# A stage-one load, a softmax and a clearing set earlier or later in a written order, and a scratch layout turned round

## The chip, the cores and the metric

The kernel runs on one core of a Trainium2 chip. The metric is the device time of one execution in microseconds; lower is better. Five engines work from queues of their own and in order: TensorE (PE; its weight loads are listed apart as PEld), VectorE (DVE), ScalarE (ACT), GpSimd (POOL) and the sync engine (SP), which here issues every DMA. An engine whose next instruction waits stands still, and so does everything behind that instruction in its queue.

## The reference

Three layers, one after the other, in float32:

```python
X = np.fft.rfft(x, axis=1)                                   # x: 8 batches, 3072 tokens, 256 channels
y = np.fft.irfft(X * (filt_r + 1j * filt_i)[None], n=3072, axis=1)
h = y.reshape(24576, 256) @ w_in                             # 256 -> 2048
z = (h / (1 + np.exp(-h))) @ w_out                           # SiLU, 2048 -> 256
logits = z @ phi                                             # 32 slots = 8 experts x 4
d = softmax(logits, axis=0)                                  # over all 24576 tokens
slot = d.T @ z
slot_out = [np.maximum(slot[e] @ w1[e], 0) @ w2[e] for e in range(8)]
out = softmax(logits, axis=1) @ slot_out                     # "combine"
```

## The kernel before

The 24576 tokens are worked in 48 chunks of 512, six to a batch. A chunk's main work is 16 hidden blocks: `hidden` (six matmuls into `ph`), `act` (ACT makes `g` with SiLU) and `turn` (DVE transposes `g` into `X`). From `g` come the logits (`pl`), from the logits an online softmax over all tokens (`soft0` to `soft3`), whose exponentials `e` go through DRAM (`spread0` stores `ed`, `spread1` loads it as `E`, line 669). `dsum` multiplies `E` with `X` into four PSUM banks (`pd`), and `update` on DVE adds them to `acc` (line 688), which frees the banks. Every four chunks a second, per-token softmax for the combine is made: `cprep` (DVE), `cexp` (ACT), `cfin` (DVE, lines 707 to 712, then a store of `cT`, line 714).

Beside these chunks the Fourier convolution of the next batch is worked in stages by `fft_plan(b, t0)`, during the six chunks of batch b-1:

- stage one, 12 steps u: `load1` (x and a piece c of the matrix), `split1` (ACT copies c into `ch`, line 286; DVE and POOL split both into high and low parts, lines 287 to 291), `mat1` (`pa`), and stores into a first scratch `s1`. The first `split1` stands in the last chunk of batch b-2, just before that chunk ends;
- stage two, four visits Q: `load2` reads `s1` as `a`, `mat2` makes `px`, ACT, DVE and POOL multiply with the filters f into y;
- stage three, `mat3` (`pb`), `out3` copies it to `eb` and `store2` writes it to a second scratch `s2` (line 265);
- stage four per chunk: `load3` reads `s2` as b (lines 540 to 542), `fly` adds and subtracts its halves on DVE, `mat4` makes `py`, and `out4` the tokens `yT` that `hidden` starts from.

Batch 0 has its own function, `fft_first`, before everything else.

Nothing schedules this: every step is put into a list with a time, `at(t, step)`, in which one hidden block is 1 and a chunk 16. The list is sorted and written out, and each engine's queue follows it (`manual_schedule`). Two times per chunk gather the small matmuls: `VIS1` = 1.9 (`pb`, the second half of the logits, `px`) and `VIS3` = 10.9 (`pd`, the first half of the logits, `py`). The instructions after that list, the tail with the experts and the output, are placed by the framework; so is the memset of the tile `sim` (line 883). A tile pool's tag has a number of buffers (`BUFS`), and a load waits until the buffer it gets is free. `px`, `pb`, `py` and `pd` share three PSUM banks (`pf`) with others.

## Time and profile before

| | us |
|---|---|
| median of 3 runs | 2019.61 (2015.79 to 2022.84) |
| the profiled execution | 2024.79 |
| its span, first to last instruction | 2023.0 |
| PE busy | 1872.3 |
| DVE busy | 1298.3 |
| ACT busy | 951.4 |
| POOL busy | 339.2 |
| mean granted TensorE clock | 0.951 of full speed |

The span is what the profile covers; the 1.8 us between it and the execution's own time lie before and after. Busy time of the engines overlaps. A granted clock of 1.00 is 2.4 GHz and 0.50 is 1.2 GHz, the two levels that the records show; a value between is a mixture of both within the stretch.

### The profile page before, as it was taken

The page shows a single profiled execution, that of the slowest core. Times are in us where ns is not written, and L with a number is a line of the kernel's source. Part 1 is how long each engine was busy: PE and PEld are TensorE (multiplying, and loading weights), DVE is VectorE, ACT ScalarE, POOL GpSimd, SP SyncE. Part 2 cuts the span into 40 slices and gives each one's busy share as a digit, 9 for nine tenths or more (in the row PEclk, how much of TensorE's full clock was granted, in tenths as well). Part 3 has the DMA queues.
Part 4 walks back from the last instruction along what each step waited for, and adds up shares of the span by engine and source line. Part 5 has one row for each costly group of instructions (what it writes and reads, how often), then busy time and mean ns, then how long its engine had stood idle before and what let it go on. Part 6 is the DMA issues. An engine that isn't in the chain of part 4 may idle for free. (4 is left out here: it accounts for less than half of the span.)

```text
span 2023.0 us, 49877 instructions
## 1 busy us (share of the span) xinstructions
PE 1872.3 (93%) x21108; PEld 1401.2 (69%) x21108; DVE 1298.3 (64%) x2207; ACT 951.4 (47%) x1816; POOL 339.2 (17%) x248
## 2 busy tenths in 40 slices
PE   4569999999999999999999999999999998999975
PEld 2158777877777777767776777767776776787643
DVE  5776665767676676767576675766576675555443
ACT  3444563554544554545544644544544544444323
POOL 3652220221121121221121211211121120000000
PEclk7679999999999999999999999999999999999996
DMA  9746442454254333553344524543254333301569
GB/s 277 212 157 185 112 113 81 144 135 118 58 178 124 92 97 96 166 134 81 90 145 125 126 63 127 155 114 80 77 159 124 95 94 106 108 24 46 182 240 386
DMA packets 196159, 264.36 MB, mean 131 GB/s; under 512 B 18784, under 2 KB 145120, under 8 KB 191712
## 3 DMA queue, kind: packets, MB, share of 16 engines
q1 hardware_dynamic: 195936, 261.17, 43.5%
q8 instruction: 166, 2.72, 0.6%
q14 instruction: 57, 0.47, 0.1%
HBM read 177.80 MB, written 83.30 MB: 129 GB/s over the span
## 5 line engine op out<-in xcount | busy, mean ns | idle before, releaser
L61 PE MATMUL ph<-yT,w_hl 128*128 128x512 f32 x4608 | 1107.3, 396 | 8.5 <-ACT g L594 6.9
L61 PEld LDWEIGHTS ph<-yT,w_hl 128*128 128x128 f32 x4608 | 859.3, 190 | 215.1 <-issue 28.3
L604 DVE STREAM_TRANSPOSE X<-g 128x512 f32<-128x512 f32 x768 | 521.0, 697 | 238.5 <-ACT g L594 238.1
L594 ACT ACTIVATE g<-ph 128x512 f32<-128x512 f32 x768 | 454.0, 607 | 347.5 <-PE ph L61 294.8
L237 POOL TENSOR_TENSOR sw<-sw,f 128x512 f32<-128x512 f32 x128 | 179.0, 1419 | 762.4 <-DMA ed<-e 230.0
L572 ACT ACTIVATE yT<-py 128x512 fp32r<-128x512 f32 x96 | 57.4, 598 | 361.2 <-PE py L61 361.2
L61 PE MATMUL pd<-X,E 32*32 32x512 f32 x6144 | 223.9, 604 | 3.0 <-issue 1.8
L61 PEld LDWEIGHTS pl<-g,wp 128*32 128x32 f32 x6144 | 164.4, 110 | 76.5 <-issue 58.9
L61 PE MATMUL pl<-g,wp 128*32 128x128 f32 x6144 | 193.2, 276 | 6.2 <-issue 6.0
L291 POOL TENSOR_TENSOR xh<-x,xh 128x512 fp32r<-128x512 f32 x84 | 111.5, 1328 | 495.2 <-DVE xh L290 426.1
L61 PEld LDWEIGHTS pd<-X,E 32*32 32x32 f32 x6144 | 119.5, 103 | 78.5 <-issue 41.8
L688 DVE SCALAR_TENSOR_TENSOR acc<-acc,nm,pd 128x512 f32<-128x512 f32 x188 | 126.9, 736 | 23.9 <-PE pd L61 23.9
L573 DVE TENSOR_TENSOR yT<-py,yT 128x512 fp32r<-128x512 f32 x96 | 66.3, 691 | 60.9 <-ACT yT L572 60.9
L61 PE MATMUL py<-d,b 128*128 128x128 f32 x416 | 72.6, 302 | 30.5 <-DVE acc L688 17.0
L361 DVE TENSOR_TENSOR y<-y,sw 128x512 f32<-128x512 f32 x112 | 98.1, 916 | 0.0
L61 PE MATMUL pa<-xh,ch 128*128 128x256 f32 x504 | 77.6, 288 | 18.2 <-ACT wp L146 9.8
L61 PE MATMUL px<-a,em 24*32 24x512 f32 (+1 forms) x1072 | 71.1, 642 | 23.6 <-DMA a<-s 17.6
L61 PEld LDWEIGHTS pa<-xh,ch 128*128 128x128 f32 x504 | 72.5, 193 | 28.6 <-ACT wp L146 10.0
L287 DVE TENSOR_TENSOR ch<-c,ch 128x256 fp32r<-128x256 f32 x84 | 42.8, 509 | 75.3 <-ACT ch L286 74.7
L226 ACT ACTIVATE sw<-px,sg 128x256 f32<-128x256 f32 x128 | 64.2, 501 | 47.1 <-DVE y L232 30.0
L61 PEld LDWEIGHTS py<-d,b 128*128 128x128 f32 x416 | 62.2, 214 | 34.8 <-DVE acc L688 18.6
L234 DVE TENSOR_TENSOR y<-px,f 128x512 f32<-128x512 f32 x120 | 78.7, 675 | 10.3 <-ACT sw L227 8.8
(126 smaller groups left out, 1305.9 us busy)
## 6 DMA issues: line engine op xcount, KB each, us to landing
f<-in_filt_dram SPq DMA_DIRECT2D x128, 256.0 KB
x<-in_x_dram SPq DMA_DIRECT2D x96, 256.0 KB
a<-s SPq DMA_DIRECT2D x128, 192.0 KB
s<-eb SPq DMA_DIRECT2D x128, 192.0 KB
out_dram<-ots SPq DMA_DIRECT2D x40, 512.0 KB
d<-in_dmat_dram SPq DMA_DIRECT2D x48, 256.0 KB
wt<-in_w_dram SPq DMA_DIRECT2D x12, 1024.0 KB
E<-ed SPq DMA_DIRECT2D x188, 64.0 KB
```

What stands on the lines that cost most here:

```text
L61: T.matmul(o, lhsT=l, rhs=r, start=start, stop=stop)
L226: A.activation(sw[:, 0, :], p[:, 1, :], AF.Copy, scale=sg[:, s:s + 1])
L234: V.tensor_tensor(y, p, f[:, 0, :].unsqueeze(1).to_broadcast([P, 2, CH]), op=ALU.mult)
L237: G.tensor_tensor(sw, sw, f[:, 1, :].unsqueeze(1).to_broadcast([P, 2, CH]), op=ALU.mult)
L287: V.tensor_tensor(ch[:, 1], c, ch[:, 0], op=ALU.subtract)
L291: G.tensor_tensor(h[:, 1, :], tf, h[:, 0, :], op=ALU.subtract)
L361: V.tensor_tensor(y, y, st.pop(("sw", Q, U)), op=ALU.add)
L572: A.activation(y[:, half, 0, :], py, AF.Copy)
L573: V.tensor_tensor(y[:, half, 1, :], py, y[:, half, 0, :], op=ALU.subtract)
L594: A.activation(g, pht.pop((c, m)), AF.Silu)
L604: V.transpose(xt[c][:, m].rearrange("p b j -> p (b j)"), gt[c, m])
L688: V.scalar_tensor_tensor(out=acc[:, :, a, :], in0=acc[:, :, a, :], scalar=mrun[c][:, 3:4], in1=p, op0=ALU.mult, op1=ALU.add)
```

## The change

Four things are changed, and the order of some steps with them.

1. In `fft_plan`, for all batches from 1 on, the first three `load1` are set nine, eight and seven times before the first `mat1`, the later ones up to seven before their own; c gets four buffers in place of two, and the tag `ev` one in place of two. `mat1` of steps 5, 6 and 7 move by up to a block.
2. The first visit of stage two (`tx`) of batches 2 to 7 moves from `t0 + 22.9` to `t0 + 27.1`, behind the `pd` and `py` of that time, as batch 1 has it already; its `load2` comes half a block earlier.
3. The combine softmax: `cfin` gets one of three places by its chunk, `cprep` another place at the end of a batch, and `cexp` is issued in whichever `soft2` comes next. The memset of `sim` gets a written place (`clear_sim`).
4. `s2` gets the layout of `s1`: `store2` writes 8 KB in one run per partition, `load3` reads pieces of 1 KB where it read 2 or 3 KB.

```diff
-            ld=3, c=2, ch=2, xh=2, ev=2, a=1, f=2, sw=1, y=2, ev8=1, bl=1, bp=1, dl=1, wt=3)
+            ld=3, c=4, ch=2, xh=2, ev=1, a=1, f=2, sw=1, y=2, ev8=1, bl=1, bp=1, dl=1, wt=3)
...
-        s2t[b] = s2 = dram.tile([64, 2, NJ, CH], F32, tag="s2", name=f"s2_{b}")
+        s2t[b] = s2 = dram.tile([NJ, 16, 4, 2, CH], F32, tag="s2", name=f"s2_{b}")
...
-            k = 16 * Q + 4 * U
-            DQ.dma_start(s2[k:k + 4].rearrange("k c r e -> r (k c) e"),
-                         ev[S * U:S * U + NJ].rearrange("r q c e -> r (q c) e"))
+            DQ.dma_start(s2[:, 4 * Q + U].rearrange("r q c e -> r (q c e)"),
+                         ev[S * U:S * U + NJ].rearrange("p q c e -> p (q c e)"))
...
-            t1, tx = [t0 + d for d in (-4.3, -3.1, -1.9, -0.7, 2.6, 4.1, 5.6, 7.1, 11.5, 12.6, 13.7, 14.8)], t0 + 22.9
-        at(t1[0] - 6, begin)
+            t1, tx = [t0 + d for d in (-4.3, -3.1, -1.9, -0.7, 2.6, 4.2, 6.4, 8, 11.5, 12.6, 13.7, 14.8)], t0 + 27.1
+        at(t1[0] - 10, begin)
...
-            at(max(t - 6, ts[u - 2] + 0.4) if u > 1 else t - 6, load1, u)
+            at(max(t - 7, ts[u - 3] + 0.4) if u > 2 else t1[0] - 9 + u, load1, u)
...
-            at(t1[-1] + 4.5 if Q == 0 else tp + 2, load2, Q)
+            at(t1[-1] + 4 if Q == 0 else tp + 2, load2, Q)
...
-        dma = DQ.dma_start(t[:, 0:n, :], s2.rearrange("k c r e -> (k c) r e")[:, r0:r0 + n, :])
+        dma = DQ.dma_start(t[:, 0:n, :], s2.rearrange("r u q c e -> (u q c) r e")[:, r0:r0 + n, :])
...
-            dma = DQ.dma_start(t[i::2, n:4, :], s2[:, 1 - i, r1:r1 + 4 - n, :])
+            dma = DQ.dma_start(t[i::2, n:4, :], s2.rearrange("r u q c e -> (u q) c r e")[:, 1 - i, r1:r1 + 4 - n, :])
...
-        if c % 4 == 0 and c // 4 - 1 in csm:
-            cexp(c // 4 - 1)
+        for k in sorted(csm.keys() - cdone):
+            cexp(k)
...
+    def clear_sim():
+        tail["sim"] = tail["tp"].tile([P, 2, NE * 36], F32, tag="sim", name="sim")
+        V.memset(tail["sim"], 0.0)
...
+    at(t + 40, clear_sim)
...
-            at(t3 + 4 if last else t1 + 11.2, cprep, c // 4)
+            at(t3 + 4 if last else t1 + (11.2 if (c + 1) % CPB else 19.1), cprep, c // 4)
...
-                at(t1 + 16 + 7.2, cfin, c // 4)
+                at(t1 + {1: 43.8, 3: 27.8, 5: 19.1}[(c + 2) % CPB], cfin, c // 4)
```

What this does to the queues, at three places. In the rows the numbers after a tile's name are its batch (or chunk) and step; the last one only counts tiles.

On SP, at the end of chunk 5, where stage one of batch 2 begins; before:

```order
L265 DMA s2_1_670<-eb_1_3_3019 24x8x256 x4
L653 DMA ed_4_3088<-e_4_3062 128x128
L669 DMA E_4_3110<-ed_4_3088 32x4x128 x4
L540 DMA b_6_3116<-s2_1_670 128x768
L542 DMA b_6_3116<-s2_1_670 64x256 x2
L278 DMA x_2_0_3122<-in_x_dram 128x2x256
L280 DMA c_2_0_3124<-in_cmat_dram 128x256
L278 DMA x_2_1_3136<-in_x_dram 128x2x256
L280 DMA c_2_1_3138<-in_cmat_dram 128x256
L531 DMA d_6_3140<-in_dmat_dram 128x512
L278 DMA x_2_2_3177<-in_x_dram 128x2x256
L280 DMA c_2_2_3179<-in_cmat_dram 128x256
```

And in the change:

```order
L264 DMA s2_1_648<-eb_1_3_3021 24x2048 x4
L277 DMA x_2_0_3079<-in_x_dram 128x2x256
L279 DMA c_2_0_3081<-in_cmat_dram 128x256
L652 DMA ed_4_3094<-e_4_3064 128x128
L277 DMA x_2_1_3097<-in_x_dram 128x2x256
L279 DMA c_2_1_3099<-in_cmat_dram 128x256
L277 DMA x_2_2_3111<-in_x_dram 128x2x256
L279 DMA c_2_2_3113<-in_cmat_dram 128x256
L716 DMA cT_86<-lall_0_1314 128x512
L668 DMA E_4_3130<-ed_4_3094 32x4x128 x4
L539 DMA b_6_3136<-s2_1_648 128x3x256
L541 DMA b_6_3136<-s2_1_648 64x256 x2
```

The loads of x and c for three steps, and the store `cT` of the combine softmax, now stand between the store of s2 and the load of E; before they stood behind E and b.

On DVE, in the same chunk (`X_5` are its turns, `cm_0` and `ct_0` the combine softmax, `ch` and `xh` the first split); before:

```order
L604 STREAM_TRANSPOSE X_5_2994<-g_5_6_3142 128x512
L604 STREAM_TRANSPOSE X_5_2994<-g_5_7_3152 128x512
L287 TENSOR_TENSOR ch_2_0_3162<-c_2_0_3124,ch_2_0_3162 128x256
L290 CAST xh_2_0_3165<-x_2_0_3122 128x512
L707 TENSOR_REDUCE cm_0_2951<-ct_0_2949 128x16
L708 TENSOR_SCALAR cm_0_2951<-cm_0_2951 128x16
L709 RECIPROCAL cm_0_2951<-cm_0_2951 128x16
L710 TENSOR_TENSOR ct_0_2949<-ct_0_2949,cm_0_2951 128x512
L712 STREAM_TRANSPOSE lall_0_1314<-ct_0_2949 128x512
L604 STREAM_TRANSPOSE X_5_2994<-g_5_8_3168 128x512
L555 SCALAR_TENSOR_TENSOR bp_6_3188<-b_6_3116,sg_79 128x256
```

And in the change:

```order
L603 STREAM_TRANSPOSE X_5_2994<-g_5_2_3085 128x512
L603 STREAM_TRANSPOSE X_5_2994<-g_5_3_3101 128x512
L709 TENSOR_REDUCE cm_0_2951<-ct_0_2949 128x16
L710 TENSOR_SCALAR cm_0_2951<-cm_0_2951 128x16
L711 RECIPROCAL cm_0_2951<-cm_0_2951 128x16
L712 TENSOR_TENSOR ct_0_2949<-ct_0_2949,cm_0_2951 128x512
L714 STREAM_TRANSPOSE lall_0_1314<-ct_0_2949 128x512
L603 STREAM_TRANSPOSE X_5_2994<-g_5_4_3121 128x512
L603 STREAM_TRANSPOSE X_5_2994<-g_5_5_3140 128x512
L603 STREAM_TRANSPOSE X_5_2994<-g_5_6_3152 128x512
L603 STREAM_TRANSPOSE X_5_2994<-g_5_7_3162 128x512
L286 TENSOR_TENSOR ch_2_0_3172<-c_2_0_3081,ch_2_0_3172 128x256
```

The softmax's closing steps went from behind the first `ch` and `xh` to a place four turns earlier.

On PE, around the first `px` of batch 2 in chunk 7 (its last rows, then the hidden blocks up to `pd`); before:

```order
L61 MATMUL px_2_02_4089<-a_2_0_4036,em_77 32x512
L61 MATMUL px_2_03_4090<-a_2_0_4036,em_77 32x512
L61 MATMUL px_2_00_4087<-a_2_0_4036,em_77 32x256 x3
L61 MATMUL ph_7_7_4112<-yT_7_3834,w_hl_75 128x512 x6
L61 MATMUL ph_7_8_4129<-yT_7_3834,w_hl_75 128x512 x6
L61 MATMUL ph_7_9_4152<-yT_7_3834,w_hl_75 128x512 x6
L61 MATMUL ph_7_10_4172<-yT_7_3834,w_hl_75 128x512 x6
L61 MATMUL pd_6_0_4186<-X_6_3478,E_6_4065 32x512 x4
```

And in the change, the rows from `py` of the same chunk to the beginning of `px`:

```order
L61 MATMUL py_8_0_4238<-d_8_4081,bp_8_4117 128x128 x2
L61 MATMUL py_8_0_4238<-d_8_4081,b_8_4065 128x128 x2
L61 MATMUL py_8_1_4243<-d_8_4081,bp_8_4117 128x128 x2
L61 MATMUL py_8_1_4243<-d_8_4081,b_8_4065 128x128 x2
L61 MATMUL ph_7_11_4253<-yT_7_3834,w_hl_75 128x512 x6
L61 MATMUL px_2_00_4260<-a_2_0_4017,em_77 32x256
```

`px` stood four hidden blocks ahead of `pd`, and now comes one block behind `py`.

## Rows read from the trace of the kernel before

The stretches are named after where they lie: A goes from `pd` of a batch's chunk 4 to `pd` of its chunk 5, B from there to `pd` of the next chunk 0, C from there to `pd` of chunk 1. Rows of windows read: stretch, its us, then busy us of PE, PEld, DVE, ACT and POOL with their instructions, the granted clock, the DMA share and GB/s.

**Rows 1.** Part 1 of the page: busy us (share of span) xinstructions.
```profile
PE 1872.3 (93%) x21108; PEld 1401.2 (69%) x21108; DVE 1298.3 (64%) x2207; ACT 951.4 (47%) x1816; POOL 339.2 (17%) x248
```

**Rows 2.** TensorE's waits: line, waited for, total us, times, longest.
```profile
PE py L61 <- DVE acc L688: 17.4, 8, 4.8
...
PE py L61 <- DMA b<-s: 12.2, 1, 12.2
```

**Rows 3.** Six stretches A, two shown and the sum: us, busy us, clock, DMA.
```profile
336.40:382.01 45.61, 40.72 (x417) 33.07 (x416) 32.57 (x68) 21.48 (x44) 11.40 (x9) 0.93 0.51 160
...
560.41:600.88 40.47, 38.66 (x417) 30.93 (x417) 30.13 (x63) 21.49 (x44) 11.42 (x9) 1.00 0.56 175
...
sum 261.22, PE 239.84 PEld 193.71 DVE 188.12 ACT 129.14 POOL 68.47; mean PE 39.97 PEld 32.28 DVE 31.35 ACT 21.52 POOL 11.41
```

**Rows 4.** A stretch of the last batch, same view.
```profile
1733.89:1766.07 32.18, 32.18 (x369) 25.40 (x368) 17.73 (x30) 13.96 (x24) 0.00 (x0) 1.00 0.32 101
```

**Rows 5.** TensorE's timeline, one `pa` in stage one: start, us, engine, line, op.
```profile
573.57 0.87 PE L61 MATMUL pa<-xh,ch 128*128 128x256 f32 x6
574.28 2.88 PE L61 MATMUL ph<-yT,w_hl 128*128 128x512 f32 x12
```

**Rows 6.** Timeline of four engines around 336 us; in brackets idle, releaser.
```profile
329.32 3.09 DVE L604 STREAM_TRANSPOSE X<-g 128x512 f32<-128x512 f32 x5 [2.20 <-ACT g L594]
...
330.48 1.91 SPq L669 DMA_DIRECT2D E<-ed  x4
...
334.80 0.60 SPq L280 DMA_DIRECT2D c<-in_cmat_dram  x1
...
336.40 4.46 PE L61 MATMUL pd<-X,E 32*32 32x512 f32 x128
...
338.56 0.42 ACT L286 ACTIVATE ch<-c 128x256 fp32r<-128x256 f32 x1 [5.53 <-DMA c<-in_cmat_dram]
...
339.68 0.68 DVE L707 TENSOR_REDUCE cm<-ct 128x16 f32<-128x512 f32 x1
...
342.21 0.71 DVE L712 STREAM_TRANSPOSE lall<-ct 128x512 f32<-128x512 f32 x1
...
346.97 0.80 PE L61 MATMUL py<-d,b 128*128 128x128 f32 x2 [4.22 <-DVE acc L688]
```

**Rows 7.** The sum over the six stretches B, same view as rows 3.
```profile
sum 249.77, PE 243.50 PEld 179.32 DVE 166.44 ACT 117.62 POOL 49.34; mean PE 40.58 PEld 29.89 DVE 27.74 ACT 19.60 POOL 8.22
```

**Rows 8.** TensorE's timeline, first `px` of batch 3.
```profile
633.81 4.37 PE L61 MATMUL px<-a,em 24*32 24x512 f32 x36 [0.50 <-DMA a<-s]
```

**Rows 9.** Two stretches C: batch 1 and batch 3.
```profile
192.97:232.92 39.95, 38.73 (x477) 27.32 (x476) 27.29 (x44) 21.33 (x44) 11.13 (x8) 1.00 0.62 147
645.65:680.75 35.10, 35.10 (x439) 26.27 (x438) 25.71 (x40) 18.62 (x36) 7.16 (x6) 1.00 0.42 107
```

**Rows 10.** TensorE's timeline inside stretch C of batch 1.
```profile
199.37 1.08 PE L61 MATMUL pl<-g,wp 128*32 128x128 f32 x32 [0.88 <-issue]
...
215.41 2.11 PE L61 MATMUL pb<-y,gm 32*32 32x512 f32 x22 [0.34 <-DVE y L361]
```

**Rows 11.** Two stretches from `pd` of a chunk 3 to the next.
```profile
975.13:1008.43 33.30, 33.30 (x401) 25.71 (x400) 17.62 (x30) 14.73 (x26) 0.00 (x0) 1.00 0.21 54
1660.31:1701.71 41.40, 35.41 (x401) 26.92 (x400) 22.15 (x40) 16.45 (x29) 0.00 (x0) 0.92 0.30 92
```

**Rows 12.** VectorE's timeline, the memset.
```profile
1687.75 0.54 DVE L883 MEMSET sim<- 128x576 f32 x1 [5.59 <-DMA s<-eb]
```

**Rows 13.** Windows inside a store of s2 and in the output.
```profile
772.00:776.00 4.00, 4.00 (x19) 3.33 (x18) 0.41 (x2) 3.94 (x7) 0.00 (x0) 1.00 0.73 172
1960.00:2000.00 40.00, 29.03 (x276) 20.72 (x274) 21.18 (x35) 17.59 (x34) 0.00 (x0) 0.75 1.01 397
```

**Rows 14.** Timeline of a chunk's middle: fly of b, and `py`.
```profile
682.27 0.75 DVE L555 SCALAR_TENSOR_TENSOR bp<-b,sg 128x512 f32<-128x512 f32 x1 [1.96 <-DMA b<-s]
...
687.26 0.71 PE L61 MATMUL py<-d,bp 128*128 128x128 f32 x4
```

More of the change, by code (lines that the diff above doesn't have):

```diff
@@ L699, in cprep @@
         csm[k] = (t, cm)
+    cdone = set()
     def cexp(k):
+        cdone.add(k)
         t, cm = csm[k]
@@ L880, in fftconv_moe_softmoe @@
         mm(pT[:, h, :], sib[:, h * P:h * P + P], fold[:, 0:S], True, True)
-    sim = tp.tile([P, 2, NE * 36], F32, tag="sim", name="sim")
-    V.memset(sim, 0.0)
+    sim = tail["sim"]
     V.tensor_copy(sim.rearrange("p h (e x) -> p h e x", x=36)[:, :, :, 0:4],
```

## The prediction

> **What bounds the kernel now.** I read the page's first part, then TensorE's waits, then its timeline, and from that the stretches between one chunk's token sums and the next (the names `pd`, which every chunk has once). PE is busy for 93% of the span [rows 1], so a gain can only come out of PE's idle time, out of matmuls that run slowly, or out of work that disappears; this change removes no matmul. The list of waits [rows 2] puts 17.4 us on `py` behind `acc` and 12.2 us on the very first `py` behind `b`, and it is misleading in one respect: it counts idle time, not what a wait costs. For that I compare stretches. A chunk of the last batch, where no FFT runs any more, takes 32.18 us from `pd` to `pd` at full clock with PE busy throughout [rows 4]. That is the floor. A stage-one step `pa` put between two hidden blocks adds 574.28 - 573.57 = 0.71 us [rows 5].
>
> Stage one of each of batches 2 to 7 begins near the end of a chunk 5, two batches ahead. Three stretches matter for each: A, from `pd` of chunk 4 to `pd` of chunk 5, with eight `pa`; B, from there to `pd` of the next chunk 0, with four `pa` and the first `px`; C, the one after. The floor of A is 32.18 + 8 x 0.71 = 37.86. The six A sum to 261.22 us [rows 3], 261.22 - 6 x 37.86 = 34.1 over. The first shown has a clock of 0.93, the second 1.00: where the wait is long the clock falls to the lower level as well, and the whole excess of the first (7.75 us) is 1.8 times its wait of 4.22. The floor of B is 32.18 + 4 x 0.71 = 35.02; the six sum to 249.77 [rows 7], 39.6 over, and that includes the first `px` itself.
>
> **Why A is late** [rows 6]. SP issues the E loads from 330.48 and the first c only at 334.80. ACT, which works in order, stands 5.53 us in front of its first `ch` until 338.56, and all its `g` behind that stand too. DVE then has `ch`, `xh`, the closing of a combine softmax (from 339.68 to 342.21 + 0.71, 3.2 us), the turns of the late `g` and the fly of b before the update of `acc`, although `pd` ended at 336.40 + 4.46 = 340.86. `py` needs the banks which that update frees: 346.97, 4.22 us late. Batches 2, 4 and 6 have the softmax there, the other three only the late c.
>
> **The change, part by part.**
> - First x and c ahead of E, and the softmax ahead of `ch`. c is issued six to seven us earlier, so ACT's stand goes, and DVE has its 3.2 us of softmax behind it before `pd` ends. What is late next: E. On SP six loads now stand between the e store and E; one x is 0.60 and one c 0.60 at most [rows 6], with the store's own issue before them, so E is ordered some 2.5 us later. In batches 2, 4 and 6 the store of the softmax (cT) stands ahead of E as well, and SP waits there for DVE. DVE begins its turns at 329.32, the softmax comes after two of five (3.09 / 5 = 0.62 each): 330.6, and takes 2.5 to 3.2 us: 333.1 to 333.8. With cT's and E's issue (1.91) E is fully ordered at about 335.5 to 336.1. The c row took 338.56 - 334.80 = 3.8 us from issue to use in a full queue; E's four parts then land between about 336 and 339, and `pd` wanted them at 336.40. Bounds 0 and 2.5 us, I take 1.0 for three batches, and 0.3 everywhere for what I don't see: 3 x 1.0 + 6 x 0.3 = 4.8. A gains 34.1 - 4.8 = **29.3** (this holds the sixth `pa`, now one block later, too).
> - First `px` joined. In B, PE had to wait for a (0.50 us in the row) and then ran 36 small matmuls in 4.37 us [rows 8]; a is now ordered before f and used nine us later. The combine softmax that was prepared in the middle of B in three of the batches (`cprep`) goes into the next chunk. I leave 0.3 a batch: B gains 39.6 - 1.8 = **37.8**. But the work comes back in C. Batch 1 has had this very order all along: `py`, one hidden block, `px`. Its C took 39.95 against 35.10 for one that has no first `px` in it [rows 9], 4.85 more, of which 0.88 is an issue wait in `pl` that isn't the visit's. That leaves 3.97: 1.83 of matmuls, about 1.6 because `pb` comes before its products y are ready [rows 10] (POOL's four cross products are the chain), and 0.5 unexplained. Bounds 3.5 and 4.85, I take 3.97: C loses 6 x 3.97 = **23.8**.
> - Clearing moved. The memset of the `sim` tile stands in DVE's queue in front of an online-softmax step, and there waits 5.59 us for a store that still reads the memory it clears [rows 12]; behind it stand the softmax, ACT's exp and every `g`. That stretch takes 41.40 us, one of the same kind 33.30 [rows 11]. Its new place is two chunks later, in front of one turn, when the last such store is long done; 0.54 us of DVE beside a busy PE costs nothing there. Gain **8.1**.
> - 8-KB runs. A store of s2 moves 4 x 192 KB at 172 GB/s with a DMA share of 0.73 in 1-KB pieces; the output, in pieces of 3 to 4 KB, runs at 397 at 1.01 [rows 13]. Per busy engine that is 14.7 and 24.6 GB/s. At the second rate 786 KB take 2.7 us in place of 4.6. In the loop that is hidden, since everything behind it has slack or is counted above. In the first batch it is exposed: nothing runs while the first `py` waits for store and load [rows 2]. Against the 1.9 us stands the load of b, in 1-KB pieces now: 524 KB at 14.7 x 16 = 235 GB/s take 2.2 us, at the better rate 1.3, so up to 0.9 back. Bounds -1.9 and +0.9; I take a gain of **1.0**. The row shows a store that never uses more than three quarters of the engines. The Trainium skill (DMA: Bandwidth & Descriptors, Why a DMA increments its semaphore by 16 and not by 1) says the number of engines is the largest up to 16 that divides the outer size on both sides; with 24 partitions that is 12, before and after. The trace agrees (0.73 is close to 12/16). By that rule alone the longer runs would leave the store as it is and this term at zero, the sum one us smaller.
> - The finishing steps of the other softmaxes move to places where DVE has its turns alone: nothing. One `ev` buffer in place of two: it is used once in 16 blocks, nothing.
>
> **Sum.** 29.3 + 37.8 - 23.8 + 8.1 + 1.0 = 52.4 us, off the profiled execution's 2024.79: 1972.4. That execution lies 5.2 us above the median of the runs (2019.61); part of it is issue waits on PE which the change does not touch. I take the same 52.4 off the median: **1967**.
>
> **Rivals.**
> - E becomes the wait (16%). For it: E's order behind cT, which waits for DVE. Against: c and x are out of the queue by then. At the late bound, 2.5 us of waiting, times the 1.8 of [rows 3] for the clock, is 4.5; less the 1.0 counted, 3.5 x 3 = 10.5: 1978.
> - The joined visit costs what it saves (5%): if y is late by 14.0 / 6 = 2.3 us more than in batch 1, B and C cancel (37.8 - 23.8 = 14.0): 1981. Against it stands batch 1, with the same tiles, banks and engine order; for it, that batch 1's neighbours are not wholly the same.
> - The loads don't come earlier (5%): x needs one of three `ld` buffers, which the filters of the visit before also use; if SP stands there, everything behind stands, and A keeps its excess: 1967 + 29.3 = 1996. Against: those filters are consumed some ten blocks earlier.
> - Slower (4%): the loads of b from the new layout. Each piece of a partition is 1 KB, with 128 KB from one to the next. If that read is slow, `py` waits in every chunk. b's fly starts at 682.27 after 1.96 us of waiting for it, takes 1.5, and `py` comes at 687.26 [rows 14]: 3.5 us of slack. A load that takes up to 3.5 us longer costs nothing; to eat 52.4 us and 6 more it must be late by 58 / 46 = 1.3 us beyond that in each of 46 chunks, so take about 4.8 us more than now: 2026. At 14.7 GB/s per engine it takes 0.9 us more, far from that; the first scratch is read with the same distance between partitions and no row shows it slow. The Trainium skill (DMA: Bandwidth & Descriptors, Latency and other measured facts) warns of row distances that are large powers of two, but its figures start to fall above 512 KiB, so by it 128 KB loses nothing; no run here shows the larger ones.
>
> **How the numbers follow.** The forecast has 70%. Its own terms at their better ends (E 0, C 3.5 each, nothing left over) give 52.4 + 3 + 2.8 + 3.6 + 0.9 = 62.7: 1957; the five us by which the runs differ widen that to 1952. At the other side the first two rivals together give 1992; they need not fall together, so I stop at 1990, which leaves the last two rivals and some rest outside. A measurement of this kernel tells 0.3% (6 us) from no change. Faster: the forecast and the first three rivals, 96%, less 3% for a mixture that ends within 6 us of 2019.6: 93%. Same 3%, slower 4%.
>
> **What would show it.** In the new profile: ACT's wait for c gone from the borders and `py` within one us of `pl`'s end, A near 38 to 39 at clock 1.00; B near 35 with no `px` in it; C near 39 with a short wait of `pb` for y; the stretch with the memset at 33.3; b's store shorter. Wrong: `pd` waiting for E at batches 2, 4 and 6, A still over 42, C over 41, or `py` waiting for b or its fly in the middle of a batch.

## The result, and the profile after

The changed kernel takes 1972.01 us (median of 4 runs, 1969.01 to 1972.46) against 2019.78 (4 runs, 2015.79 to 2022.84): a ratio of 0.9761, 95% interval 0.9742 to 0.9781, so 47.8 us less. The forecast was 1967, in 1952 to 1990. The profiled execution took 1971.93 us, 52.86 less than that of before; 52.4 had been worked out. The sum came out, but its terms did not all: two were too large, and one cost was set against a base that was too low.

Part 1 of the page, as [rows 1]: TensorE does the same number of matmuls in 23 us less busy time and 53 us less span.

```profile
PE 1848.9 (94%) x21108; PEld 1385.5 (70%) x21108; DVE 1287.9 (65%) x2207; ACT 951.0 (48%) x1816; POOL 340.5 (17%) x248
```

TensorE's waits, as [rows 2]: of the eight waits of `py` for `acc`, three are left. `a` is waited for twice where it was eight times, once of it in the prologue. A long wait of `pd` for E, 3.1 us, is new; before had two of at most 0.4.

```profile
PE px L61 <- DMA a<-s: 15.9, 2, 15.6
...
PE py L61 <- DVE acc L687: 4.6, 3, 2.6
PE pl L61 <- issue: 4.0, 5, 2.6
...
PE pd L61 <- DMA E<-ed: 3.1, 1, 3.1
```

The stretches, with the columns of [rows 3]. First A of batches 3 and 4 and the sum of the six, then the sum of the six B, then C of batch 3 and the sum of the six C, last the two stretches around the clearing.

```profile
555.80:594.26 38.46, 38.46 (x418) 31.19 (x417) 27.60 (x60) 19.79 (x40) 10.36 (x8) 1.00 0.48 151
771.52:814.35 42.83, 40.23 (x418) 32.79 (x417) 28.06 (x61) 19.78 (x40) 11.51 (x9) 0.96 0.47 144
...
sum 237.72, PE 233.09 PEld 189.23 DVE 166.75 ACT 118.72 POOL 65.62; mean PE 38.85 PEld 31.54 DVE 27.79 ACT 19.79 POOL 10.94
...
sum 212.11, PE 211.68 PEld 168.48 DVE 145.08 ACT 98.92 POOL 25.50; mean PE 35.28 PEld 28.08 DVE 24.18 ACT 16.49 POOL 4.25
...
629.36:668.70 39.34, 38.75 (x477) 27.10 (x476) 27.56 (x44) 21.84 (x45) 11.15 (x8) 1.00 0.54 128
...
sum 234.48, PE 231.66 PEld 162.70 DVE 165.36 ACT 129.48 POOL 66.95; mean PE 38.61 PEld 27.12 DVE 27.56 ACT 21.58 POOL 11.16
...
1608.47:1645.28 36.81, 33.68 (x402) 25.67 (x402) 21.92 (x39) 17.05 (x30) 0.00 (x0) 0.98 0.33 102
1645.28:1680.17 34.89, 34.89 (x368) 27.21 (x368) 16.92 (x29) 13.37 (x23) 0.00 (x0) 0.92 0.37 110
```

A and B end where they were to end, except A of batches 4 and 6 (42.83 and 40.37). C is 39 as forecast. But the six C of before, of which the prediction took a single one at 35.10 [rows 9] for all, add up to 219.89, with one of 39.45 among them (before, the same view):

```profile
1316.16:1355.61 39.45, 36.90 (x440) 27.60 (x439) 25.12 (x39) 18.63 (x36) 7.35 (x6) 0.96 0.43 98
...
sum 219.89, PE 213.44 PEld 159.15 DVE 151.88 ACT 112.06 POOL 43.32; mean PE 35.57 PEld 26.53 DVE 25.31 ACT 18.68 POOL 7.22
```

| difference of the two profiles, us gained | predicted | measured |
|---|---|---|
| A, six stretches (261.22 to 237.72) | 29.3 | 23.5 |
| B, six (249.77 to 212.11) | 37.8 | 37.7 |
| C, six (219.89 to 234.48) | -23.8 | -14.6 |
| the two stretches around the clearing (73.58 to 71.70) | 8.1 | 1.9 |
| up to the first `pd` | 1.0 | 1.1 |
| batch 1's four stretches (143.43 to 147.08) | 0 | -3.6 |
| the stretches from chunk 1 to 3 of later batches (425.90 to 418.05) | 0 | 7.8 |
| all else | 0 | -0.9 |
| sum | 52.4 | 52.9 |

The border at which stage one of batch 4 begins, the worst of those left, as [rows 6]; timeline of the changed kernel:

```profile
763.01 1.11 SPq L279 DMA_DIRECT2D c<-in_cmat_dram  x1
...
767.60 0.71 DVE L714 STREAM_TRANSPOSE lall<-ct 128x512 f32<-128x512 f32 x1
...
768.04 0.41 ACT L285 ACTIVATE ch<-c 128x256 fp32r<-128x256 f32 x1
...
768.34 0.33 SPq L716 DMA_DIRECT2D cT<-lall  x1
768.76 1.82 SPq L668 DMA_DIRECT2D E<-ed  x4
771.11 1.13 SPq L541 DMA_DIRECT2D b<-s  x2
...
771.52 4.98 PE L61 MATMUL pd<-X,E 32*32 32x512 f32 x128
...
777.41 0.48 DVE L554 SCALAR_TENSOR_TENSOR bp<-b,sg 128x256 f32<-128x256 f32 x1 [5.47 <-DMA b<-s]
...
780.23 2.68 DVE L687 SCALAR_TENSOR_TENSOR acc<-acc,nm,pd 128x512 f32<-128x512 f32 x4
...
780.99 0.80 PE L61 MATMUL py<-d,b 128*128 128x128 f32 x2 [2.60 <-DVE acc L687]
```

ACT's `ch` waits for nothing now, and the softmax is done before `pd` begins. E, ordered at 768.76, is there when `pd` wants it at 771.52. What is late is b, ordered behind it: DVE stands 5.47 us in front of the fly, the update of `acc` stands behind the fly, and `py` waits for that update as before, 2.60 us where it was 3.39 at this border. So the wait of before has a new first cause: SP stands at the store cT until DVE has made `lall` (767.60 + 0.71), and orders E and b only behind it.

The clearing itself waits for nothing at its new place (VectorE, as [rows 12]). But two chunks earlier, where it used to stand, `pd` now waits for E (SP's and TensorE's timeline):

```profile
1714.40 0.54 DVE L744 MEMSET sim<- 128x576 f32 x1
```

```profile
1635.91 0.34 SPq L740 DMA_DIRECT2D wo<-wos  x1
...
1638.91 0.32 SPq L716 DMA_DIRECT2D cT<-lall  x1
1639.32 2.03 SPq L668 DMA_DIRECT2D E<-ed  x4
...
1645.28 7.21 PE L61 MATMUL pd<-X,E 32*32 32x512 f32 x128 [3.11 <-DMA E<-ed]
```

In front of E stands `wo`, the 2 MB of the experts' weights. `wo` stood there before, too. But the memset [rows 12] stood in front of the last operation on `nm`, which ACT's exp needs, and PE waited for the late `g` (before; VectorE's, then TensorE's timeline):

```profile
1688.21 0.10 DVE L627 TENSOR_SCALAR nm<-nm 128x1 f32<-128x1 f32 x1
```

```profile
1692.84 8.94 PE L61 MATMUL ph<-yT,w_hl 128*128 128x512 f32 x30 [5.99 <-ACT g L594]
```

SP had ordered E by 1694.12, 7.6 us before the late `pd` at 1701.71, and E was there in time. In the change 0.8 us are left between the two.

### The profile page after: what moved, and what is told of

The parts are those of the page before. It is cut to its first block, busy times and chain, and to the rows that moved or that the text cites. A ratio compares the mean times of both kernels' runs of the same rounds, so it can differ in the third digit from the quotient of the medians.

```text
span 1970.2 us, 49869 instructions
## 1 busy us (share of the span) xinstructions
PE 1848.9 (94%) x21108; PEld 1385.5 (70%) x21108; DVE 1287.9 (65%) x2207; ACT 951.0 (48%) x1816; POOL 340.5 (17%) x248
## 5 line engine op out<-in xcount | busy, mean ns | idle before, releaser
L61 PE MATMUL ph<-yT,w_hl 128*128 128x512 f32 x4608 | 1096.2, 393 | 2.1 <-ACT g L593 1.7
L603 DVE STREAM_TRANSPOSE X<-g 128x512 f32<-128x512 f32 x768 | 515.6, 694 | 206.0 <-ACT g L593 205.6
L360 DVE TENSOR_TENSOR y<-y,sw 128x512 f32<-128x512 f32 x112 | 104.8, 975 | 0.0
L61 PE MATMUL py<-d,b 128*128 128x128 f32 x416 | 68.4, 290 | 17.9 <-DMA b<-s 11.6
L554 DVE SCALAR_TENSOR_TENSOR bp<-b,sg 128x512 f32<-128x512 f32 (+1 forms) x48 | 34.9, 727 | 69.9 <-DMA b<-s 69.3
L633 ACT ACT_TABLE_LOAD x48 | 61.6, 1283 | 37.2 <-DVE nm L626 26.2
L61 PE MATMUL pb<-y,gm 32*32 32x512 f32 (+1 forms) x1072 | 70.1, 627 | 9.2 <-DVE y L464 5.6
```

The source lines that it names most:

```text
L61: T.matmul(o, lhsT=l, rhs=r, start=start, stop=stop)
L360: V.tensor_tensor(y, y, st.pop(("sw", Q, U)), op=ALU.add)
L603: V.transpose(xt[c][:, m].rearrange("p b j -> p (b j)"), gt[c, m])
L633: A.activation(t[:, 0], L, AF.Exp, bias=nm[:, 1:2], accum_out=nm[:, 2:3])
```

## The experiments

Each kernel but the last is the changed one with the edit shown; A, B, C and single stretches are read from its profile. Medians of different kernels come from different runs, so a difference of 3 or 4 us between two of them is not told from none.

**The 2-MB load later.** `wo` three blocks later in SP's order, behind E, b and d.

```diff
+    def load_wo():
         DQ.dma_start(tail["wo"], wos)
...
+    at(t + 5, load_wo)
```

> The change with one edit: the 2-MB load of wo (the expert stage's matrix, wos) is issued after the loads of E, b and d of chunk 40/41 and no longer ahead of them. In the changed kernel the stretch from pd 39 to pd 40 takes 36.81 us and the next 34.89, with 3.11 us of waiting for E. Theory: E lies behind those 2 MB on the DMA engines; with wo later the two stretches take 33.3 and 32.2, 6.2 us less, so about 1966 us. Rival: E is late because SP stands at the store cT until DVE has closed the combine softmax; then the stretches stay within 1 us and the time stays at 1972.

1970.61 us, ratio 0.9746 (0.9711 to 0.9780). `pd` no longer waits, and 1608.47:1645.28 of the change has become (windows of this kernel; the third row is one stretch later):

```profile
1609.73:1643.35 33.62, 33.59 (x402) 25.64 (x401) 21.92 (x39) 16.45 (x29) 0.00 (x0) 1.00 0.16 42
1643.35:1676.64 33.29, 32.69 (x370) 25.76 (x369) 16.69 (x29) 13.96 (x24) 0.00 (x0) 1.00 0.57 182
1676.64:1709.92 33.28, 32.74 (x369) 25.67 (x368) 17.43 (x29) 13.96 (x24) 0.00 (x0) 1.00 0.34 100
```

The three together are 100.2 where they were 104.0. That E stood behind `wo` is shown; the rest of the floor is given back one chunk later, where PE is idle 0.6 us a stretch.

**The store of the combine softmax later.** cT behind E, b and d at the borders.

```diff
-            DQ.dma_start(cT[k], o)
+            co[k] = o
...
+    def cstore(k):
+        DQ.dma_start(cT[k], co.pop(k))
...
+                    at(tf + (3.2 if (c + 2) % CPB == 5 else 0), cstore, c // 4)
```

> The change with one edit: the store cT of the combine softmax is issued after E, b and d at the batch borders where it stood ahead of them. Stretches A of the changed kernel: 39.26, 42.83 and 40.37 us for batches 2, 4 and 6, 38.4 for the other three; in the long ones DVE stands up to 5.47 us in front of the fly of b. Theory: b is late because SP stands at cT and orders E and b behind it; with cT later the three A come to 38.4 to 38.8, 6 to 7 us less in all, about 1965 us. Rival: b is late because its load, in 1-KB pieces, is slow or queues behind x and c; then A falls by no more than the 0.5 to 1 us by which SP is earlier, 2 us in all: 1970.

1966.80 us, ratio 0.9734 (0.9692 to 0.9775). A of batch 4 fell from 42.83 to 38.63, batch 6 from 40.37 to 38.89, and PE is busy through all six:

```profile
771.53:810.16 38.63, 38.63 (x417) 31.57 (x416) 28.08 (x61) 19.76 (x40) 11.51 (x9) 1.00 0.52 158
...
sum 233.56, PE 233.56 PEld 190.40 DVE 166.99 ACT 118.27 POOL 65.52; mean PE 38.93 PEld 31.73 DVE 27.83 ACT 19.71 POOL 10.92
```

So it was cT, which waits for DVE, that held b and E; with it out of the way, nothing in A waits.

**The old layout of s2.** The lines of `store2` and `load3` go back with it.

```diff
-        s2t[b] = s2 = dram.tile([NJ, 16, 4, 2, CH], F32, tag="s2", name=f"s2_{b}")
+        s2t[b] = s2 = dram.tile([64, 2, NJ, CH], F32, tag="s2", name=f"s2_{b}")
...
```

> The change without its new layout of the second scratch s2 (stores in 1-KB pieces and loads of b in pieces of 2 to 3 KB again). Theory of the prediction: the store takes 4.6 in place of 2.7 us and the load of b up to 0.9 less, which only the first batch shows: the first pd 1.0 us later, all else equal, 1973. Rival one: the engines of a store are set by its 24 partitions and the layout does nothing: 1972 and the first pd within 0.3 us. Rival two: the 1-KB pieces are what makes b late at the borders: A of batches 2, 4 and 6 come down by 1 to 3 us each and the time falls by 3 to 7.

1976.31 us, ratio 0.9773 (0.9737 to 0.9808): 4.3 more, with intervals that overlap. The first `pd` comes at 192.63, with the new layout at 191.88 to 193.56 in eleven profiles: the term of 1.0 us cannot be seen. Three microseconds inside a store, with nothing else on the queues, first in the changed kernel and then here:

```profile
911.12:914.12 3.00, 3.00 (x28) 2.36 (x13) 2.35 (x7) 2.54 (x6) 0.00 (x0) 1.00 0.73 158
```

```profile
911.46:914.46 3.00, 3.00 (x28) 2.36 (x13) 2.35 (x7) 2.55 (x6) 0.00 (x0) 1.00 0.63 143
```

Eight times as much in one run gives a tenth more rate, 158 for 143 GB/s, and the engines' share stays at about three quarters (0.61 to 0.76 in the 28 stores of the loop). The 172 GB/s of [rows 13], put there to 1-KB runs, are those of a window that also holds the store of `ed`, ordered at 774.19; the 2.5 us of the same store ahead of it have 141 at 0.62. The six A are 237.4 in this kernel, as with the new layout, so it is not the pieces of 1 KB that make b late. The Trainium skill (DMA: Bandwidth & Descriptors, Why a DMA increments its semaphore by 16 and not by 1) gives 12 of 16 engines for 24 partitions; the 0.73 of the 8-KB runs agrees.

**The first visit at its old place, or the loads in their old order, or both.**

```diff
-            t1, tx = [... 14.8)], t0 + 27.1
+            t1, tx = [... 14.8)], t0 + 22.9
...
-            at(t1[-1] + 4 if Q == 0 else tp + 2, load2, Q)
+            at(t1[-1] + 4.5 if Q == 0 else tp + 2, load2, Q)
```

> The change with the first visit of stage two at its old place for batches 2 to 7 (px four blocks ahead of pd, a ordered half a block later), all else as changed. Theory: the visit by itself costs what it cost before, 4 to 5.4 us each and 4.6 of slow clock in two of them, 31 us together in stretches B, and gives 24 back in C: about 7 us slower than the change, 1979. Rival: px only waited because a and its neighbours were late on SP and DVE; with the loads earlier the visit takes about 2.3 us each, B grows by 14 and C falls by 24: 10 us faster than the change, 1962.

```diff
-        at(t1[0] - 10, begin)
+        at(t1[0] - 6, begin)
...
-            at(max(t - 7, ts[u - 3] + 0.4) if u > 2 else t1[0] - 9 + u, load1, u)
+            at(max(t - 6, ts[u - 2] + 0.4) if u > 1 else t - 6, load1, u)
```

> The change with x and c of stage one loaded in the old order again (behind E and b), all else as changed, the combine softmax early. Theory one, the late c and the softmax each have a share: with c late ACT stands again, but DVE has the softmax behind it, so all six stretches A look like those of batches 3, 5 and 7 before, 40.5 to 43: 10 us slower than the change, 1982. Theory two, the loads did it all: A goes back to the 261 us of before, 23 us slower, 1995.

And with both edits:

> The changed kernel with both the first visit and the loads of x and c at their old places; what is left of the change is the softmax, the clearing and the layout of s2. Undone alone, the loads gave 1989.5 and the visit 1991.7, each 17 to 20 above the change's 1972.0, while the whole change is worth 47.8. Theory one: the two gains lie in different stretches and add, so both undone give 1972.0 + 17.5 + 19.7 = 2009, and the rest of the change is worth some 10 us. Rival: each covers part of what the other does (a late c at the border delays the visit, too, and each takes away some of the same low clock), so both undone give more, about 2017, and the rest of the change is worth the 2 or 3 us that undoing the clearing and the layout gave (1.9 and 4.3).

| | loads early | loads in old order |
|---|---|---|
| visit joined | 1972.0 | 1989.5 (0.9852, 0.9815 to 0.9889) |
| visit at its old place | 1991.7 (0.9846, 0.9810 to 0.9882) | 2011.6 (0.9942, 0.9924 to 0.9961) |

The earlier loads are worth 17.5 or 19.9 us, the joined visit 19.7 or 22.1, and together 39.6: they add. Alone, the visit is worth more than either theory on it had, and the loads lie between the two on them. By the stretches, undoing the visit puts 33.6 us back into B (245.7) and takes 16.1 off C, and undoing the loads puts 20.8 back into A (258.5) and leaves B at 210.5. With both undone, the theory that the gains add (2009) is nearer than its rival (2017). What is left of the change is worth 10.9 (2022.5 of before in those runs, less 2011.6); by the two profiles 7.8 of it lie in B (249.8 to 241.9), from which the preparation of the softmax has gone, and 1.7 around the clearing. With the visit at its old place, the first `px` still waits for a, and the blocks behind it run in part at the lower level (kernel with the old visit; 24 `ph` take 8.50 us at a mean granted clock of 0.65, against 5.74 for 24 in a row at full clock):

```profile
407.08 2.60 PE L61 MATMUL px<-a,em 24*32 24x512 f32 x34 [0.76 <-DMA a<-s]
409.61 8.50 PE L61 MATMUL ph<-yT,w_hl 128*128 128x512 f32 x24
```

With both undone, the border is late again, in batches 2, 4 and 6 by more than in before, since c now stands behind cT as well as behind E and b (batch 4, ACT's, then TensorE's timeline; in before ACT waited 4.89 us there and `py` 3.39):

```profile
789.48 0.42 ACT L285 ACTIVATE ch<-c 128x256 fp32r<-128x256 f32 x1 [11.02 <-DMA c<-in_cmat_dram]
```

```profile
795.41 0.80 PE L61 MATMUL py<-d,b 128*128 128x128 f32 x2 [5.74 <-DVE acc L687]
```

The six C are 218.4 and 221.4 in the two kernels with the old visit, as 219.9 in before: that C lies well over the floor comes with that order and is no chance of one profile. The last part of this section tells what the nine us are.

**The combine softmax at its old place.**

```diff
-            at(t3 + 4 if last else t1 + (11.2 if (c + 1) % CPB else 19.1), cprep, c // 4)
+            at(t3 + 4 if last else t1 + 11.2, cprep, c // 4)
...
-                at(t1 + {1: 43.8, 3: 27.8, 5: 19.1}[(c + 2) % CPB], cfin, c // 4)
+                at(t1 + 16 + 7.2, cfin, c // 4)
```

> The change with cprep and cfin of the combine softmax at their old places, all else as changed, x and c early. Theory one: 3.2 us of DVE in front of the update of acc make py late by 1 to 2 us in batches 2, 4 and 6, and cprep in the middle of B costs 1.9 us again in batches 3, 5 and 7: 10 us slower, 1982. Theory two: the softmax hurt only because ACT and DVE were late with c; now DVE has room for it, and cT no longer stands ahead of E and b: the time stays or falls by up to 4 us, 1968 to 1972.

1971.86 us, ratio 0.9766 (0.9725 to 0.9808): no difference. In the stretches it is two that cancel: A falls to 231.5, since cT is not in front of E and b (moving cT alone gave 233.6), and B rises to 217.4. With c early, the softmax's 3.2 us in front of the update no longer hurt.

**The clearing without a written place.**

```diff
-    at(t + 40, clear_sim)
...
-    sim = tail["sim"]
+    sim = tp.tile([P, 2, NE * 36], F32, tag="sim", name="sim")
+    V.memset(sim, 0.0)
```

> The change with the memset of the sim tile where the framework put it, in front of a step of the online softmax. Theory of the prediction: its wait costs 8.1 us, 1980. Theory after the profile of the change: the wait of pd for E behind the 2-MB load of wo stood behind it all the time, so the stretches 39 to 41 go from 71.7 back to about 73.6 us and no further: 1974.

1973.90 us, ratio 0.9775 (0.9738 to 0.9813), 1.9 more, which is not told from none. The run does not bring the clearing back to where it stood: the framework now set the memset one operation later, behind the last one on `nm` (first row). It waits for the store again, but ACT's exp, at 1631.68, and the `g` don't wait with it. The two stretches are 72.9 us against 71.7, and E is late at the same place as in the change (VectorE's, then TensorE's timeline of this kernel).

```profile
1630.17 0.15 DVE L626 TENSOR_SCALAR nm<-nm 128x1 f32<-128x1 f32 x1
1635.52 0.54 DVE L889 MEMSET sim<- 128x576 f32 x1 [5.20 <-DMA s<-eb]
```

```profile
1646.18 7.25 PE L61 MATMUL pd<-X,E 32*32 32x512 f32 x128 [4.20 <-DMA E<-ed]
```

**The last two y of the first visit earlier.** Their two adds on DVE go ahead of two turns.

```diff
-                at(t + ((3.6, 3.7, 6, 6.1) if Q == 0 else (4.1, 4.2, 8.3, 8.4))[U], add2, Q, U)
+                at(t + ((3.6, 3.7, 4.005, 4.006) if Q == 0 else (4.1, 4.2, 8.3, 8.4))[U], add2, Q, U)
```

> The change with one edit: in the first visit of stage two DVE adds the last two products y right behind the first two, ahead of two turns of X and no longer behind them. Theory one: of the 3.97 us that each C pays, 1.2 to 1.5 are pb waiting for y because those turns stand ahead of the adds; C falls to 37.4 to 38.1 in seven batches: 9 us faster, 1963. Theory two: POOL's four products are the chain, the adds wait for POOL and hold up the turns: C stays at 38.8 to 39.3, the time at 1972 or some us above.

1965.89 us, ratio 0.9729 (0.9685 to 0.9773). In the change `pb` stops for y in C (first fence), here it runs through (second), and C of batch 3 is 38.15 in place of 39.34; the six fall from 234.5 to 229.8, about half of what theory one had for them.

```profile
434.59 2.11 PE L61 MATMUL pb<-y,gm 32*32 32x512 f32 x22 [0.35 <-DVE y L360]
```

```profile
433.86 2.36 PE L61 MATMUL pb<-y,gm 32*32 32x256 f32 x38
```

**The three shifts together, and the same with the old softmax.** `wo` later, cT later, adds earlier; then `wo` later, adds earlier and the softmax's two lines of before.

> The changed kernel with three more shifts together: the 2-MB load of wo three blocks later, the store cT behind E, b and d at the borders, and the adds of the last two y of the first visit ahead of two turns. Alone these gave 1970.6, 1966.8 and 1965.9 against 1972.0. Theory one: each takes away a wait of its own (39 to 40; A of batches 2, 4 and 6; C), so the gains add: 1972.0 - 1.4 - 5.2 - 6.1 = about 1959, by the stretches (3.8 + 4.2 + 4.7) also about 1959. A falls to 233.6, C to about 229.8, 39 to 41 to about 67. Rival: the two last gains lie within what runs of one kernel differ by, and partly take the place of one another: 1964 to 1967.

1958.01 us (1957.78 to 1960.18), ratio 0.9680 (0.9661 to 0.9700): the gains add, 14.0 us under the change. This is the best version of the case. A is 233.27 and the two stretches around the clearing are back at the floor:

```profile
1600.72:1634.34 33.62, 33.59 (x402) 25.63 (x401) 21.92 (x39) 16.45 (x29) 0.00 (x0) 1.00 0.21 51
1634.34:1666.51 32.17, 32.17 (x369) 25.22 (x368) 17.16 (x30) 13.96 (x24) 0.00 (x0) 1.00 0.56 186
```

> As the kernel with three shifts, but with the combine softmax at its old place in place of the later store cT: cT then is stored well behind E and b by itself. Theory one: the late cT is what the softmax's new place cost, so putting the softmax back does the same as moving cT, and this runs within 4 us of the kernel with three shifts (about 1959). Rival: the softmax at its old place delays acc in A and the prepared part stands in B (B was 217.42 against 212.11 with it), so it is 5 or more slower (1964 or above).

1969.29 us, ratio 0.9728 (0.9705 to 0.9750): 11 more. Three of the six B, those that hold the preparation of the softmax, take 37.2 us in place of 35.05 to 35.57 (windows of this kernel):

```profile
594.10:631.34 37.24, 35.84 (x393) 27.95 (x392) 26.91 (x51) 17.01 (x31) 4.22 (x3) 1.00 0.45 134
```

The six B are 217.7 against 212.1, 5.6 us; of the rest, 3.5 lie in the stretches from chunk 1 to 2, and their cause is open. So the new place of the softmax pays, once cT is not in front of E.

**Where the nine us in C were.** In before, the longest stretch C (30 to 31) has 2.55 us in which TensorE stands for nothing that the profile names. TensorE's timeline; then a window just ahead of it; then a DMA queue from 1322 to 1323 (packets, MB, share):

```profile
1324.92 0.65 PE L61 MATMUL pl<-g,wp 128*32 128x128 f32 x7 [2.55 <-issue]
```

```profile
1321.00:1323.00 2.00, 1.38 (x49) 1.11 (x41) 2.00 (x4) 0.00 (x0) 0.00 (x0) 1.00 1.01 318
```

```profile
q8 instruction: 1, 0.02, 7.0%
```

A packet of TensorE's instructions, 16 KB, comes through the same DMA engines, at a moment at which they are full (share 1.01) of a and f for stage two; 1.3 us after it is there, `pl` goes on. The page lists 166 such packets, and TensorE has 42645 instructions in the trace (matmuls, weight loads and semaphore waits): 166.6 times 256. Numbered in order through the trace, all nine of these waits in before between 190 and 1880 us come at an instruction (the matmul or the weight load just ahead of it) whose number is 193 more than a multiple of 256. Such a place is called a border here. The waits stand in front of `pl`, `pd`, `py` and `ph`, in nine different chunks. In the change, whose order puts other matmuls at those numbers, there are five, all at 193 again. The same border, instruction 28609, in before and in the change (TensorE's timeline):

```profile
1362.23 1.83 PE L61 MATMUL pd<-X,E 32*32 32x512 f32 x2 [1.77 <-issue]
```

```profile
1328.49 1.73 PE L61 MATMUL pl<-g,wp 128*32 128x128 f32 x53 [0.49 <-issue]
```

The border moved from `pd` to `pl` with the order, and the wait moved with it. The border 27841 of the 2.55 us lies in the first `px` in the change, and nothing waits there. In all fourteen profiles of this case there are 92 such waits in that time, all at a border, and each ends 1.2 to 1.6 us after a packet has landed, in step with the count: one packet to one border.

The traces also say which borders cost something. The packet of a border starts at about the time at which TensorE passes the border before it (0.5 us after that, in the median), so it has the time of 256 instructions to arrive. Of the 2164 borders in that time 472 come after 256 instructions that were begun within 5 us, and 90 of the 92 waits are among these; where the 256 took over 8 us, at 1418 borders, there is none. Among the 472 the traffic decides: with a DMA share below 0.4 in the three us ahead, 20 of 288 wait, none of them a whole us; at 0.7 and more 41 of 100, up to 3.66 us.

In before the four C that are longer than 35.10 have one such wait each (1.46, 0.27, 2.55 and 1.65 us, 5.9 of the 9.3 us by which they are longer), and the two of 35.10 have none. The four profiles with the visit at its old place have 8.2 to 11.5 us of these waits in all, the ten with the visit joined 2.3 to 6.8.

A direct test was to be the kernel before with its borders set half a block off:

```diff
                 stage2(pxs[Q], aa[:, Q], Q)
+                for _ in range(2 if Q in (1, 2) else 0):
+                    stage2(pxs[Q], aa[:, Q], Q)
```

> The kernel before, with the stage-two matmuls of batch 0's visits 1 and 2 written two more times each: 64 more matmuls, 128 more instructions on TensorE (a matmul and its weight load each), some 2 to 4 us of work in the first 190 us; the result is the same, and nothing else moves in any queue. In the traces so far every wait of TensorE that is put down to issue comes at the same count of its instructions, 193 more than a multiple of 256, and 1.3 to 1.6 us after a 16-KB packet of an instruction queue landed. Theory one (TensorE's code comes in blocks of 256 instructions, behind the data loads): the borders now fall 128 instructions earlier in the program; the waits inside the last parts of pl near 199, 1325 and 1560 are gone from there, and those that remain stand at other matmuls, in pd, pl or ph, again at 193 more than a multiple of 256. Sizes are open: the sum of the waits was 9.5 us and may come out between 3 and 14, and the time within 8 us of before's 2020. Rival (the waits belong to those matmuls or to the traffic at that place and only look like code): they stay at the same pl matmuls, 0.9, 2.6 and 1.7 us long, now at a count of 65 over a multiple of 256.

2028.79 us, ratio 1.0020 (0.9996 to 1.0044). The edit missed its size: each of those matmuls is two on TensorE, so 128 were added and not 64, and 256 instructions, a whole block. That leaves every border at the matmul where it was, so the run can't tell the two theories apart, and what speaks against the rival is the count above, over orders that put different matmuls at a border; the count of packets went from 166 to 167, and the eleven waits are again at 193. What it does show is that the same border costs different times: the one of 2.55 us above, again with 7 `pl` left, cost

```profile
1339.55 0.42 PE L61 MATMUL pl<-g,wp 128*32 128x128 f32 x7 [0.63 <-issue]
```

and that stretch C took 36.02 in place of 39.45. The six C of this kernel sum to 214.8, so the old order loses 4 to 11 us there, by four profiles (214.8, 218.4, 219.9, 221.4).

The Trainium skill (Runtime: NRT & Kernel Launch, Instruction fetch mechanics) has the code in blocks of 16 KiB, 256 instructions, and calls the cost mostly hidden. The size agrees with the packets here. At 2072 of the 2164 borders it is hidden here, too, but not always where the DMA queues are full and `pd` and `pl`, 384 matmuls and weight loads in 6.4 us, use the code up fast. That was 9.5 us of waiting in before and 4.0 in the change, and more with the clock that falls behind it (0.96 in the stretch shown above). What a border moved on purpose would give was not tried.

This run showed something on the clearing, too. The framework set its memset behind the softmax and one turn, where it waits 0.48 us and not 5.59 and holds up no exp; and then `pd` waits for E in the old order as well (VectorE's, then TensorE's timeline). The two stretches are 72.0 us, 1.6 less than in before:

```profile
1692.94 0.54 DVE L885 MEMSET sim<- 128x576 f32 x1 [0.48 <-DMA s<-eb]
```

```profile
1702.13 7.36 PE L61 MATMUL pd<-X,E 32*32 32x512 f32 x128 [3.28 <-DMA E<-ed]
```

## Why the prediction was right, and where not

- **c in time, softmax ahead** (29.3, measured 23.5 in A; undoing the loads alone costs A 20.8 and the median 17.5 to 19.9). The mechanism is shown: undo the loads and ACT's stand and the wait of `py` are back. Its size was off, in the residual: 4.8 predicted, 237.72 - 6 x 37.86 = 10.6 measured. The step that failed was "What is late next: E". E was in time in all six A; the load behind it, b, was late, and through the fly it reached the same update and the same `py`. The cause, cT ahead of them waiting for DVE, was named, and the kernel with the later cT shows it: 4.2 us, where 3.0 had been put for E. The larger part of the miss is the floor: with cT later and PE busy throughout, the six A still lie 6.4 us over 6 x 37.86, where 0.3 each had been left (A of batch 3 takes 38.46 with no wait at a clock of 1.00). That the softmax's 3.2 us were part of the trouble was wrong once c is early. With c late it isn't shown either: with the softmax early and the loads late, `py` still waits 4.6 to 5.7 us in batches 2, 4 and 6, since cT then stands ahead of c.
- **First `px` joined, B** (37.8, measured 37.7) was right: undone alone, the visit costs B 33.6 and the place of the softmax 5.3. Right was also where it comes back: C of the change is 3.98 a batch over the floor, 3.97 predicted. Of the 1.6 that were put to `pb` before y, the earlier adds took back 0.8. What failed is the base, "39.95 against 35.10 for one that has no first `px` in it": one row stood for six that sum to 219.9, not 210.6. So the net gain in B and C is 23.1 and not 14.0, of which 17.5 are the visit's own by undoing it. The nine us between are mostly code borders, 5.9 us of waiting and the clock behind it; that moving the visit moved the a and f loads and the borders apart fits the shorter waits of the ten kernels with the joined visit, but no run shows it by itself. Of the 7.8 us in the chunks behind, 5.5 are one stretch (41.35 to 35.88) with such a wait of 1.77 in it.
- **Clearing** (8.1, measured 1.9 in the profiles; no run put the memset back in front of the exp) failed. "That stretch takes 41.40 us, one of the same kind 33.30" took the whole excess for the memset's. E's wait behind the 2 MB of `wo` lay under it and came out once the exp was in time: in the change, in the kernel without a written place and in the last one. With `wo` later as well the two stretches are 66.9 and 65.8, so the excess was there to be gained, 4.8 to 5.9 us of it behind `wo`. What the old memset costs with `wo` later was not run.
- **8-KB runs** (1.0): not seen. The 1.1 us of the table up to the first `pd` is less than eleven profiles of the new layout differ by. The rate assumed, 287 GB/s, was that of another transfer, 158 was measured; and the 172 of the old one held another store's bytes, alone it is 143 at a share of 0.63. The prediction's other reading of this term, twelve engines before and after and so nothing, was the better guide.
- **The sum, and from the profile to the median.** That the profiles differ by 52.9 where 52.4 was worked out is in part luck: A and the clearing gave 12 us less, C and the chunks behind it 17 more, and batch 1 lost 3.6, mostly to a code border at `pl` (2.61 us, 0.88 in [rows 10]). The profiled execution of before was 5 us above its median; code waits differ from profile to profile (0.8 to 3.7 us at the one border near 200 us that thirteen of them share), but what made that execution longer is not shown. "I take the same 52.4 off the median" carried them over, and the median gained 47.8 (44.2 to 52.1 by the interval). That step is the 5 us by which 1967 was too low.
- **Rivals.** Of "E becomes the wait" the half with cT came true, for b and in two of three batches (4 to 6 us of A, not 10.5). "The joined visit costs what it saves" and "the loads don't come earlier" did not happen. The read of b from the new layout is not slower by anything that reaches `py` in the middle of a batch.

## What to carry to other kernels

When a late load is moved forward, look at everything that it now stands in front of, down to the last load whose user feeds the same wait, and let no store that waits for an engine stand among them. A wait's whole excess may be credited to its removal only if the stretch is looked through for the next thing that was covered by it; and the base of a difference is the sum over all its stretches, not the cleanest one. Waits that the trace can't name deserve a count of the instruction they stand at.

## What was not expected of the hardware

- TensorE's unnamed waits are code, by all that was seen: 92 waits of 0.2 to 3.7 us in fourteen profiles, all at one place in 256 instructions, and all end 1.2 to 1.6 us after a 16-KB instruction packet has landed. 90 of them follow 256 instructions begun within 5 us, and of the 27 that are over 1 us, 22 come under a DMA share of 0.7 or more in the three us ahead. At the same border their length changes from profile to profile.
- A store from 24 partitions stays at a share of 0.73 and 158 GB/s with 8-KB runs, against 0.63 and 143 with 1-KB runs.
